# The first batch of a fused attention and MLP kernel: V by pairs, another order of steps, and copies on another engine

## The chip, the cores and the metric

The kernel runs on one core of a Trainium2 chip. A core has engines that run their own instruction streams in order: TensorE (PE in the profile; PEld is its weight load), VectorE (DVE), ScalarE (ACT), GpSimd (POOL) and SyncE (SP). They wait for each other through semaphores. Matmul results go to PSUM, which holds eight banks here; data is loaded from device memory by DMAs that POOL or SyncE issue. The metric is the device time of one execution in microseconds, as the median of several runs.

## What is computed

The reference is sparse attention, then an MLP with a squared ReLU. q, k and v are 8 x 8 x 576 x 64 (batch, head, position, channel); the first four heads look at the last 32 positions (local), the other four at the positions with the same remainder modulo 32 (strided).

```python
scores = scale * np.matmul(q, k.transpose(0, 1, 3, 2))
mask_local = (rel >= 0) & (rel < stride)
mask_strided = (rel >= 0) & (pos[None, :] % stride == pos[:, None] % stride)
scores = np.where(masks[None, :, :, :], scores, -1000000000.0)
attn = np.exp(scores - max) / sum
x = (attn @ v)                        # 4608 tokens x 512
h = x @ w_in                          # 512 x 2048
g = np.maximum(h, 0.0) ** 2
out = g @ w_out                       # 2048 x 512
```

## The kernel before, in words

Heads are worked in pairs, called units: unit u of batch b is 4b to 4b+3, the first two local, the last two strided. A unit's steps are: T, transposes of q and k on PE (TS for the strided units of the first two batches); S (`step_S`, L309), the scores with PE into four PSUM banks (two heads, called rows, by two halves of the blocks) and their exponential on ScalarE into the tile e; D (`step_D`, L405), for a local unit one part per head: e times V on PE with a column of ones beside V, a reciprocal (L434) and a product (L435) on VectorE into x_l; E (`step_E`, L438), which transposes x_l on PE and copies it to xt, the tile that the MLP reads (L464). The strided units of the first two batches use other steps in place of D and E: N (`step_N`, L378) sums e with PE and makes reciprocals with a logarithm and an exponential on ScalarE (L387, L388); O (`step_O`, L390) multiplies V by e so that the result is transposed already, and two VectorE products (L400) write xt.

The MLP takes 512 tokens at a time: `mm1` (L474) gives h for 128 columns of d_ff in four matmuls (L482), one for each 128 rows of w_in, which are the four units' channels, kk = 0 to 3; ScalarE then takes the ReLU (L488), VectorE the square (L491); `mm2` (L495) is the second matmul (L522). xt[0] and xt[1] come from the local pairs 0 and 1, xt[2] and xt[3] from the strided pairs.

No scheduler moves anything: the engines run the instructions in the order in which the program emits them (`manual_schedule`). For batch 0 that order is the list `order` in `first_steps` (L547). Each entry is a step and a number of filler matmuls (`warm`, L537) after it, whose results nobody reads. `part((kk,))` runs the matmuls of one kk for the first five column blocks of the first 512 tokens, into five banks, so that the MLP can start before all four units are done; `first_order` says which kk comes when, and in which order the first half of w_in is loaded. Later batches go by `stream_steps` (L569) and a plan of hooks, which place their loads between groups of MLP matmuls.

All early loads but the first two are on POOL's queue, in this order: q and k of unit 1 (L130), q and k of the strided units (L153), V of the local pairs (L237 for 96 of the partitions, L238 for the 32 positions before each block), V of the strided pairs (L374), and w_in (four slices at L673, then two blocks at L257). Eight semaphores serve POOL's DMAs in turn, so each issue also waits until the eighth DMA before it has landed. SyncE has its own eight.

Later in the kernel, batches 2 to 4 take their strided q and k through a cast into device memory (L165) and a transposing DMA from SyncE (L173); V of batches 2 and 3 is loaded after a small POOL copy (L605) that waits for those transposes. From batch 5 on the local q and k are loaded by SyncE (L114), cast on POOL and transposed by a DMA (L201); before that stands a DMA called hold (L609), which waits for V of batch 4.

In the list of batch 0 before the change, the part after S(2) runs: D(0,0), D(0,1), S(3), D(1,0), N(2), a filler, E(0), N(3), D(1,1), O(2), part kk=0, E(1), O(3), part kk=2, part kk=1, part kk=3.

Of the kernel before, what the change touches and what calls it, by code (L numbers as in the profile page):

```python
# [10 lines left out]
AF = mybir.ActivationFunctionType  # L11
# [3 lines left out]
def kernel(  # L15
# [9 lines left out]
    nc = tc.nc  # L25
    B, H, S, D = q.shape
# [4 lines left out]
    scale = 1.0 / (D ** 0.5)  # L31
    QL = 96
    NL = S // QL
# [25 lines left out]
    def bank(nm):  # L59
        t = banks[nm].pop(0)  # L60
        banks[nm].append(t)
        while id(t) in unread:
            run_due(lambda x: x[1] == unread[id(t)])
        return t

    unread = {}
# [3 lines left out]
    NV = 4  # L70
# [4 lines left out]
    vl_all = singles.tile([128, NV, 2, NL, VP], BF16, name="vl")  # L75
    vls = [vl_all[:, i] for i in range(NV)]
# [21 lines left out]
    st = {}  # L98

    def is_local(u):  # L100
        return units[u][1] < H // 4
# [32 lines left out]
    def cast_qk_local(u, copies, names="qk"):  # L134
        s = st[u]
        for name, copy in zip("qk", copies):
            if name not in names:
                continue
            t = qk_in.tile([QL, 6, 2, D], BF16, name=f"{name}_l")
            copy(t.rearrange("p j h d -> p h j d"),  # L140
                 s[name + "f"].rearrange("p h (j d) -> p h j d", j=6))
            s[name] = t
# [87 lines left out]
        for i in range(2):  # L230
            st.setdefault(4 * b + 2 + i, {})["vf"] = t[:, 2 * i:2 * i + 2]

    def load_v_local_sw(b):
        i = (2 * b) % NV
        t = vl_all[:, i:i + 2].rearrange("p u h t d -> p (u h t) d")[:, :, 0:D]
        src = v[b, 0:4].rearrange("h (t p) d -> p (h t) d", p=QL)
        nc.gpsimd.dma_start(out=t[32:128], in_=src)  # L237
        nc.gpsimd.dma_start(out=t[0:32, 1:4 * NL], in_=src[64:96, 0:4 * NL - 1])  # L238
        for u in range(2):
            st.setdefault(4 * b + u, {})["v"] = vls[i + u]  # L240

    def load_v_str(u, eng):
        b, p = units[u]
# [23 lines left out]
    def later(n, fn, key=None):  # L267
        pending.append((clock[0] + n, key, fn))
# [37 lines left out]
    def blk_pos(h, j):  # L306
        return NJ * (j % 2) + 4 * h + j // 2

    def step_S(u, at_once=False):  # L309
        s = st[u]  # L310
        qT, kT = s["qT"], s["kT"]
        local = is_local(u)
        w, n = (QL, NL) if local else (SP_, NJ)
        kn = 128 if local else SP_
        hn = n // 2
        e = es[u % 4]
        s["e"] = e
        pss = [[None, None], [None, None]]
        for half in range(2):
            for row in range(2):  # L320
                pss[row][half] = bank("pt")
                if u < 4:
                    bias = bias_l[:, half].rearrange("p t c -> p (t c)") if local \
                        else bias_s.rearrange("p t c -> p (t c)")
                    nc.tensor.matmul(pss[row][half][0:kn, 0:S // 2], ident[0:kn, 0:kn], bias,
                                     start=True, stop=False, skip_group_check=True)
            for i in range(hn):
                t = half * hn + i
                klo = w * t
                for row in range(2):  # L330
                    rows = slice(64 * row, 64 * row + 64)
                    if not local:
                        c0 = w * (t // 4)
                        lhsT, rhs = (a[rows, t % 4, c0:c0 + w] for a in (kT, qT))
                    else:
                        lhsT, rhs = kT[rows, klo:klo + kn], qT[rows, w * t:w * (t + 1)]
                    nc.tensor.matmul(pss[row][half][0:kn, w * i:w * (i + 1)], lhsT, rhs,  # L337
                                     start=u > 3, stop=True, skip_group_check=u < 4)

        for row in range(2):  # L340
            for half in range(2):
                unread[id(pss[row][half])] = u

        def expo(row, half):
            del unread[id(pss[row][half])]
            lo = S * row + S // 2 * half
            nc.scalar.activation(e[0:kn, lo:lo + S // 2], pss[row][half][0:kn, 0:S // 2],  # L347
                                 AF.Exp, scale=scale)

        def masks(row):  # L350
            x = e[0:kn, S * row:S * (row + 1)].rearrange("p (t c) -> p t c", c=w)
            m = mask_full if local else mask_str.to_broadcast([kn, n, w])
            nc.vector.tensor_tensor(x, x, m, op=ALU.mult)  # L353

        if u < 4:
            for half in range(2):
                for row in range(2):
                    expo(row, half)
            return
        if at_once:  # L360
            for row in range(2):
                for half in range(2):
                    expo(row, half)
            later(1, lambda: masks(0), u)
            later(2, lambda: masks(1), u)
            return
        expo(0, 0)
        later(1, lambda: expo(1, 0), u)
        later(2, lambda: expo(0, 1), u)
        later(3, lambda: (masks(0), expo(1, 1)), u)  # L370
        later(4, lambda: masks(1), u)
# [66 lines left out]
    def step_E(u):  # L438
        s = st[u]
        b, p = units[u]  # L440
        x = s["x"]
        local = is_local(u)
        n, w = (NL, QL) if local else (NJ, SP_)
        if not local and b >= XD:
            xd = dram.tile([S, 2 * D], BF16, name="x_d")
            nc.sync.dma_start(out=xd.rearrange("(p j) c -> p (j c)", j=NJ), in_=x.rearrange("p n d -> p (n d)"))
            nc.sync.dma_start_transpose(out=xt[p][:, b * S:(b + 1) * S], in_=xd)
            st.pop(u)
            return
        if local and b >= XB:  # L450
            nc.sync.dma_start_transpose(
                out=xt[p][:, b * S:(b + 1) * S].rearrange("c (t q) -> c t q", q=QL),
                in_=x.rearrange("p n d -> p (n d)"))
            st.pop(u)
            return
        px = bank("pt").bitcast(BF16)[:, 0:S]
        for t in range(n):
            nc.tensor.transpose(px[:, w * t:w * (t + 1)],  # L458
                                x[:, 2 * t:2 * t + 2, :].rearrange("p h d -> p (h d)"),
                                ident[0:w, 0:w])  # L460
        dst = xt[p][:, b * S:(b + 1) * S]
        copy = nc.scalar.copy if u < 12 else nc.vector.tensor_copy
        if local:
            copy(dst, px)  # L464
        else:
            copy(dst.rearrange("c (p j) -> c p j", j=NJ),
                                  px.rearrange("c (j p) -> c p j", j=NJ))
        st.pop(u)
# [64 lines left out]
    S_ = lambda u, at_once=False: (lambda: step_S(u, at_once or relaxed[0]))  # L533
    D_ = lambda u, part: (lambda: step_D(u, part))
    E_ = lambda u: (lambda: step_E(u))

    def warm(n):  # L537
# [3 lines left out]
                nc.tensor.matmul(pw, idle[:, 0:128], idle, start=True, stop=True)  # L541

    idle = xt[0][:, T - 512:T]
    first_order = (0, 2, 1, 3)
    NP = 5

    def first_steps():  # L547
        t, n, o = T_, (lambda u: lambda: step_N(u)), (lambda u: lambda: step_O(u))
        a, b, c, d = first_order

        def part(kks, ffs=range(NP)):
            for ff in ffs:
                mm1(0, ff, kks, first_order, None if ff < 2 else "py" if ff == 2 else "pt")

        cast1 = lambda nm: (lambda: cast_qk_local(1, (nc.vector.tensor_copy,) * 2, nm))
        v_, s_ = nc.vector.tensor_copy, nc.scalar.copy
        ts = lambda nm, half, copy: (lambda: step_TS(0, nm, half, copy))
        order = [(t(0, "q"), 2), (t(0, "k"), 2), (cast1("q"), 0), (cast1("k"), 0), (S_(0), 0),
                 (t(1, "q"), 0), (t(1, "k"), 1), (bias_strided, 0), (ts("q", 0, v_), 0), (ts("q", 1, v_), 0), (S_(1), 1),
                 (ts("k", 0, v_), 0), (ts("k", 1, s_), 1), (S_(2), 0), (D_(0, 0), 0), (D_(0, 1), 0), (S_(3), 0),  # L560
                 (D_(1, 0), 0), (n(2), 1), (E_(0), 0), (n(3), 0), (D_(1, 1), 0),
                 (o(2), 0), (lambda: part((a,)), 0), (E_(1), 0), (o(3), 0), (lambda: part((b,)), 0),
                 (lambda: part((c,)), 0), (lambda: part((d,)), 0)]
        return order

    def has_T(u):
# [37 lines left out]
    def load_v_local_gated(b):  # L604
        nc.gpsimd.tensor_copy(vl_all[64:65, (2 * b) % NV, 0, 0, 0:1], came[b])  # L605
        load_v_local_sw(b)
# [60 lines left out]
                            NEG, -NEG, op0=ALU.mult, op1=ALU.add)  # L667
    nc.vector.memset(bias_l[0:32, 0, 0], -NEG)
    load_qk_str(0, "k", room=w_out_b[:, 4:10, :])
    load_v_local_sw(0)  # L670
    load_v_str_first(0)
    for kk in first_order:
        nc.gpsimd.dma_start(out=w_in_b[:, kk, 0:1024], in_=w_in_v[:, kk, 0:1024])  # L673
# [97 lines left out]
    ts = lambda nm, half: (lambda: step_TS(1, nm, half, nc.scalar.copy if nm == "q" else nc.vector.tensor_copy))  # L771
# [82 lines left out]
```

## Time and profile before

| what | us |
|---|---|
| median of 5 runs | 308.51 |
| lowest and highest run | 308.26, 310.08 |
| profiled execution, its own time | 310.71 |
| its span, first to last instruction | 309.0 |
| PE busy, 15.0 to 18.0 / 18.0 to 20.2 / 20.2 to 23.0 | 2.84 / 1.84 / 2.64 |
| VectorE busy in the same stretches | 1.94 / 1.58 / 1.20 |
| ScalarE busy in the same stretches | 2.80 / 1.91 / 0.58 |

The granted TensorE clock was 1.00 throughout. A line of the profile names the line of the kernel, the engine, the operation, what is written from what, and how often; in the timeline the first two columns are the start and the duration (of the whole group, if several are merged), and the bracket gives the idle time before it and what ended it. In the table of waits the columns are the total, how often, and the longest.

### The profile page before, as it was taken

How to read it: one execution, taken by the hardware profiler on the slowest of the kernel's cores; microseconds unless marked ns; L12 is line 12 of the kernel's file. 1: busy time of each engine (PE TensorE's matmuls, PEld its weight loads, DVE VectorE, ACT ScalarE, POOL GpSimd, SP SyncE). 2: the span in 40 equal slices, each digit the busy share in tenths (PEclk: the TensorE clock that was granted, in tenths of full speed). 3: DMA queues.
4: the chain of work that ended last, by engine and by line, in shares of the span. 5: the costliest groups of instructions: out<-in, count | busy, mean ns of one | idle time of the engine just before them, and what ended most of it. 6: DMA issues, size and time to landing. Idle time of an engine off the chain costs nothing.

```text
span 309.0 us, 6071 instructions
## 1 busy us (share of the span) xinstructions
PE 297.5 (96%) x2326; PEld 149.8 (48%) x2368; DVE 158.5 (51%) x405; ACT 167.3 (54%) x346; POOL 74.4 (24%) x103
## 2 busy tenths in 40 slices
PE   7899999999999999899999999999999999999995
PEld 3554464545555544445444545444444444444444
DVE  4458645478677765666477577445422222222200
ACT  3768747787667765454545565555434444444311
POOL 8653400630873022722093043000000000000000
PEclk9999999999999999999999999999999999999999
DMA  8999996999999999989999783221230001000121
GB/s 161 168 207 205 189 215 126 215 194 119 133 213 88 170 202 177 200 206 220 160 231 204 192 182 88 72 55 53 75 106 35 34 34 36 34 34 36 54 82 69
DMA packets 94118, 40.75 MB, mean 132 GB/s; under 512 B 78858, under 2 KB 87754, under 8 KB 93898
## 3 DMA queue, kind: packets, MB, share of 16 engines
q0 software_dynamic: 34528, 15.00, 39.4%
q1 hardware_dynamic: 59562, 25.37, 37.1%
q8 instruction: 18, 0.29, 0.4%
q14 instruction: 10, 0.08, 0.1%
HBM read 37.64 MB, written 13.57 MB: 166 GB/s over the span
## 4 chain that ended last, share of the span: by engine, by line
PE 76%; DMA 9%; issue 6%; POOL 3%; ACT 3%; SPq 2%; DVE 1%; POOLq 0%; DVEq 0%
PE ph L482 31%; PE py L522 25%; PE ph L522 7%; PE pt L337 3%; PE pt L422 3%; DMA q_st<-in_q_dram 2%; DMA vl<-in_v_dram 2%; DMA kTl<-k_l 2%; PE pt L482 1%; DMA kT_s<-k_d 1%; DMA vl_st<-in_v_dram 1%; PE ph L504 1%; SPq L114 1%; ACT e L347 1%; PE pt L458 1%
## 5 line engine op out<-in xcount | busy, mean ns | idle before, releaser
L482 PE MATMUL ph<-xt,w_in_b 128*128 128x512 bf16 x534 | 137.7, 379 | 1.6 <-issue 0.5
L488 ACT ACTIVATE r<-ph 128x512 bf16<-128x512 f32 x138 | 82.3, 597 | 94.1 <-PE ph L482 91.2
L491 DVE TENSOR_TENSOR g_sb<-r 128x512 bf16<-128x512 bf16 x144 | 65.8, 458 | 107.1 <-ACT r L488 106.0
L522 PE MATMUL py<-w_out_b,g_sb 128*128 128x512 bf16 x385 | 100.8, 379 | 0.9 <-issue 0.2
L482 PEld LDWEIGHTS <-w_in_b 128*128 128x128 bf16 x576 | 52.4, 98 | 55.7 <-issue 0.5
L522 PEld LDWEIGHTS <-g_sb 128*128 128x128 bf16 x560 | 50.8, 98 | 54.7 <-issue 0.4
L347 ACT ACTIVATE e<-pt 72x288 bf16<-72x288 f32 (+1 forms) x128 | 45.6, 407 | 10.9 <-PE pt L337 10.9
L522 PE MATMUL ph<-w_out_b,g_sb 128*128 128x512 bf16 x139 | 34.1, 379 | 0.2
L422 PEld LDWEIGHTS <-e 128*128 128x128 bf16 (+1 forms) x384 | 20.2, 97 | 15.0 <-issue 1.0
L435 DVE TENSOR_TENSOR x_s<-pt,rinv 72x384 bf16<-72x384 f32 (+1 forms) x36 | 18.3, 509 | 1.2
L526 ACT COPY y<-py 128x512 f32<-128x512 f32 x25 | 14.6, 586 | 7.0 <-PE py L522 6.7
L435 DVE TENSOR_TENSOR x_l<-pt,rinv 96x384 bf16<-96x384 f32 x28 | 15.5, 554 | 1.0
L353 DVE TENSOR_TENSOR e<-e,mask_str 72x576 bf16<-72x576 bf16 x28 | 14.0, 510 | 3.8 <-ACT e L347 3.7
L434 DVE RECIPROCAL rinv<-pt 96x6 f32<-96x6 f32 (+2 forms) x64 | 11.8, 184 | 6.9 <-PE pt L422 6.7
L353 DVE TENSOR_TENSOR e<-e,mask_full 128x576 bf16<-128x576 bf16 x28 | 12.6, 450 | 1.9 <-ACT e L347 1.7
L422 PE MATMUL pt<-vs,e 72*128 72x65 bf16 x192 | 12.1, 193 | 0.4 <-DVE x_l L435 0.2
L220 POOL CAST vl<-vl_st 128x768 bf16<-128x768 f32 x6 | 5.4, 904 | 29.4 <-PE ph L482 16.8
L526 ACT COPY y<-ph 128x512 f32<-128x512 f32 x9 | 5.3, 584 | 13.0 <-PE ph L522 12.8
L140 POOL CAST q_l<-q_st 96x768 bf16<-96x768 f32 x6 | 5.3, 883 | 27.6 <-ACT e L347 17.5
L422 PE MATMUL pt<-vl,e 128*128 128x65 bf16 x168 | 9.8, 193 | 0.5 <-DMA vl<-in_v_dram 0.5
L617 POOL DMA_DIRECT2D vs<-in_v_dram x12 | 9.8, 819 | 1.3 <-DMA vs<-in_v_dram 1.0
L337 PEld LDWEIGHTS <-kT_s 64*72 64x72 bf16 x256 | 6.0, 113 | 7.0 <-issue 6.6
(110 smaller groups left out, 201.5 us busy)
## 6 DMA issues: line engine op xcount, KB each, us to landing
out_dram<-y SPq DMA_DIRECT2D x35, 256.0 KB, 2.8
w_out_b<-in_moe_w_out_dram POOLq DMA_DIRECT2D x4, 512.0 KB, 15.5
q_d<-in_q_dram POOLq DMA_DIRECT2D x6, 288.0 KB, 8.9
k_d<-in_k_dram POOLq DMA_DIRECT2D x6, 288.0 KB, 9.2
q_st<-in_q_dram SPq DMA_DIRECT2D x12, 144.0 KB, 4.8
k_st<-in_k_dram SPq DMA_DIRECT2D x12, 144.0 KB, 4.5
vl_st<-in_v_dram SPq DMA_DIRECT2D x12, 144.0 KB, 3.4
v_st<-in_v_dram SPq DMA_DIRECT2D x6, 288.0 KB
```

The source lines that it names most:

```text
L337: nc.tensor.matmul(pss[row][half][0:kn, w * i:w * (i + 1)], lhsT, rhs, start=u > 3, stop=True, skip_group_check=u < 4)
L347: nc.scalar.activation(e[0:kn, lo:lo + S // 2], pss[row][half][0:kn, 0:S // 2], AF.Exp, scale=scale)
L353: nc.vector.tensor_tensor(x, x, m, op=ALU.mult)
L422: nc.tensor.matmul(po[:, n - n0, :], e[0:kn, pos(n):pos(n) + 128], rhs[0:kn, src(n), 0:D + 1], start=True, stop=True)
L434: nc.vector.reciprocal(rinv[0:w, 0:m], po[0:w, 0:m, D:D + 1])
L435: nc.vector.tensor_tensor(x, po[0:w, 0:m, 0:D], rinv[0:w, 0:m].to_broadcast([w, m, D]), op=ALU.mult)
L482: nc.tensor.matmul(ph, w_in_b[:, kk, 128 * ff:128 * (ff + 1)], xt[kk][:, 512 * c:512 * (c + 1)], start=(kk == order[0]), stop=(kk == order ...
L488: nc.scalar.activation(r, ph, AF.Relu)
L491: later(1, lambda: nc.vector.tensor_tensor(g[:, ff, :], r, r, op=ALU.mult))
L522: nc.tensor.matmul(py, g[:, ff, 128 * j:128 * (j + 1)], w_out_b[:, ff, :], start=(ff == 0), stop=(ff == 15))
L526: nc.scalar.copy(y, py)
L617: nc.gpsimd.dma_start(out=t[:, NJ * i:NJ * (i + 1), 0:D], in_=v[b, h + i].rearrange("(p j) d -> p j d", j=NJ))
```

## The change

It has four parts, all in batch 0. V of the local pairs is loaded with one pair of DMAs for unit 0 and another for unit 1, in place of one pair for both. The xt copies of E(0) and E(1) run on VectorE and not on ScalarE. `step_S` can emit the exponentials of a half at once and another step between its halves; S(3) uses this to take D(0,1) between them. The list after S(2) becomes D(0,0), S(3) half 0, D(0,1), S(3) half 1, N(2), a filler, D(1,0), E(0), a filler, D(1,1), N(3), part kk=0, E(1), O(2), part kk=1, part kk=2, O(3), part kk=3; `first_order` is (0, 1, 2, 3), for the parts and for the loads of w_in.

```diff
-    def load_v_local_sw(b):
-        i = (2 * b) % NV
-        t = vl_all[:, i:i + 2].rearrange("p u h t d -> p (u h t) d")[:, :, 0:D]
-        src = v[b, 0:4].rearrange("h (t p) d -> p (h t) d", p=QL)
+    def load_v_local_sw(b, u0=0, nu=2):
+        i = (2 * b + u0) % NV
+        t = vl_all[:, i:i + nu].rearrange("p u h t d -> p (u h t) d")[:, :, 0:D]
+        src = v[b, 2 * u0:2 * (u0 + nu)].rearrange("h (t p) d -> p (h t) d", p=QL)
         nc.gpsimd.dma_start(out=t[32:128], in_=src)
-        nc.gpsimd.dma_start(out=t[0:32, 1:4 * NL], in_=src[64:96, 0:4 * NL - 1])
-        for u in range(2):
-            st.setdefault(4 * b + u, {})["v"] = vls[i + u]
+        nc.gpsimd.dma_start(out=t[0:32, 1:2 * nu * NL], in_=src[64:96, 0:2 * nu * NL - 1])
+        for u in range(nu):
+            st.setdefault(4 * b + u0 + u, {})["v"] = vls[i + u]
...
-    def step_S(u, at_once=False):
+    def step_S(u, at_once=False, between=None):
...
-        for row in range(2):
-            for half in range(2):
+            for row in range(2):
                 unread[id(pss[row][half])] = u
...
+            if between:
+                for row in range(2):
+                    expo(row, half)
+                between(half)
+        if between:
+            return
...
-        copy = nc.scalar.copy if u < 12 else nc.vector.tensor_copy
+        copy = nc.scalar.copy if 1 < u < 12 else nc.vector.tensor_copy
...
-    first_order = (0, 2, 1, 3)
+    first_order = (0, 1, 2, 3)
...
-                 (ts("k", 0, v_), 0), (ts("k", 1, s_), 1), (S_(2), 0), (D_(0, 0), 0), (D_(0, 1), 0), (S_(3), 0),
-                 (D_(1, 0), 0), (n(2), 1), (E_(0), 0), (n(3), 0), (D_(1, 1), 0),
-                 (o(2), 0), (lambda: part((a,)), 0), (E_(1), 0), (o(3), 0), (lambda: part((b,)), 0),
-                 (lambda: part((c,)), 0), (lambda: part((d,)), 0)]
+                 (ts("k", 0, v_), 0), (ts("k", 1, s_), 1), (S_(2), 0),
+                 (D_(0, 0), 0), (lambda: step_S(3, between=lambda half: None if half else step_D(0, 1)), 0), (n(2), 1),
+                 (D_(1, 0), 0), (E_(0), 1), (D_(1, 1), 0), (n(3), 0), (lambda: part((a,)), 0), (E_(1), 0),
+                 (o(2), 0), (lambda: part((b,)), 0), (lambda: part((c,)), 0), (o(3), 0), (lambda: part((d,)), 0)]
...
-    load_v_local_sw(0)
+    load_v_local_sw(0, 0, 1)
+    load_v_local_sw(0, 1, 1)
```

More of the change, by code (lines that the diff above doesn't have):

```diff
@@ L318, in step_S, with expo @@
         pss = [[None, None], [None, None]]
+        def expo(row, half):
+            del unread[id(pss[row][half])]
+            lo = S * row + S // 2 * half
+            nc.scalar.activation(e[0:kn, lo:lo + S // 2], pss[row][half][0:kn, 0:S // 2],
+                                 AF.Exp, scale=scale)
         for half in range(2):
@@ L338, in step_S @@
                                      start=u > 3, stop=True, skip_group_check=u < 4)
-        for row in range(2):
-            for half in range(2):
+            for row in range(2):
                 unread[id(pss[row][half])] = u
[L344 to L348, printed above, removed]
+            if between:
[4 more added lines that the diff above has]
+            return
         def masks(row):
```

## The prediction

> **What bounds the kernel now.** I read the page's totals first, then the timeline of 12 to 24 us, where the changed steps run, then what the matmul engine waits for after that, then the queue behind those waits.
>
> ```profile
> span 309.0 us, 6071 instructions
> PE 297.5 (96%) x2326; PEld 149.8 (48%) x2368; DVE 158.5 (51%) x405; ACT 167.3 (54%) x346; POOL 74.4 (24%) x103
> ```
>
> PE is busy 96% of the span: whatever keeps it from starting the MLP's matmuls early is paid in full, unless a later wait takes it back. The timeline of the start:
>
> ```profile
> 10.50 0.82 DVE L191 COPY qT_s<-ph 128x576 bf16<-128x576 bf16 x2 [0.33 <-PE ph L189]
> ...
> 14.09 0.54 PE L422 MATMUL ph<-vl,e 128*128 128x65 bf16 x12
> 14.10 0.68 POOL L130 DMA_DIRECT2D q_st<-in_q_dram  x1 [0.64 <-DMA g_sb<-in_v_dram]
> ...
> 14.48 0.19 DVE L434 RECIPROCAL rinv<-ph 96x6 f32<-96x6 f32 x1 [1.70 <-PE ph L422]
> 14.71 0.55 DVE L435 TENSOR_TENSOR x_l<-ph,rinv 96x384 bf16<-96x384 f32 x1
> ...
> 17.71 0.62 ACT L464 COPY xt<-pt 128x576 bf16<-128x576 bf16 x1
> ...
> 18.39 0.59 PE L482 MATMUL ph<-xt,w_in_b 128*128 128x512 bf16 x2 [0.36 <-ACT xt L464]
> ...
> 19.81 0.45 PE L398 MATMUL pt<-e,g_sb 72*64 72x72 bf16 x16
> 19.92 0.64 ACT L464 COPY xt<-pt 128x576 bf16<-128x576 bf16 x1 [0.26 <-PE pt L458]
> 20.19 8.96 PEld L482 LDWEIGHTS <-w_in_b 128*128 128x128 bf16 x43
> 20.25 1.20 DVE L400 TENSOR_TENSOR xt<-pt,g_sb 128x288 bf16<-128x288 f32 x2 [0.67 <-PE pt L398]
> ...
> 22.36 0.59 PE L482 MATMUL ph<-xt,w_in_b 128*128 128x512 bf16 x2
> ```
>
> From 14.09 on, PE goes from one step to the next. The start-to-start distances give each step's cost on PE: D half of a local pair 0.28 (15.69 to 15.98), half of S(3) 0.60 and 0.62, N 0.36, E 0.35 (19.46 to 19.81), O 0.38, a filler matmul 0.22, a part of five matmuls 5 x 0.216 = 1.08. The steps before the last part (at 22.36) sum to 7.84 with the two D halves of pair 0 back to back at 0.38; 22.36 - 14.09 = 8.27. So only 0.43 us there is waiting, 0.36 of it for the ScalarE copy of x. **No new order can gain more than about 0.4 us here**, but it can lose. What PE waits for after 23 us:
>
> ```profile
> PE pt L337 <- DMA kTl<-k_l: 1.3, 1, 1.3
> PE pt L422 <- DMA vl<-in_v_dram: 0.5, 1, 0.5
> ```
>
> The first is at 128.83, the second at 84.87. Where they come from, in the POOL and SyncE timelines and the chain:
>
> ```profile
> 36.78 0.53 POOL L165 DMA_DIRECT2D q_d<-in_q_dram  x1
> 50.98 1.39 SPq L173 DMA_TRANSPOSE qT_s<-q_d  x1
> 76.16 0.18 POOL L605 COPY vl<-kT_s 1x1 bf16<-1x1 bf16 x1 [11.57 <-DMA kT_s<-k_d]
> 77.92 6.91 DMA vl<-in_v_dram
> 105.66 0.30 SPq L609 DMA_DIRECT2D hold<-vs  x1
> 123.55 5.24 DMA kTl<-k_l
> ```
>
> q_d lands 14.1 us after its issue, at 50.88, and the transpose goes at 50.98; the next batch repeats this (63.51 + 7.3 = 70.81, transpose 70.88; gate 76.16; V issued 77.92, landed 84.82, PE at 84.87). This chain stands on landings since the start, not on PE: if PE is late, the 0.53 us wait shrinks first, and if PE were early it would grow.
>
> **The change part by part.**
> *V pair by pair.* Two DMA issues become four, with all bytes as before. One pair's issues lie between 2 x 0.68 (a DMA of few pieces, L130) and 1.21 + 0.74 (the whole loads, L237 and L238); four cost 2.7 to 3.9 against 1.95, so POOL's later issues (V of the strided pairs, six of w_in) come 0.8 to 1.95 later; I take 1.3, in the middle. The landings: K of the strided pairs 10.1, V 12.4 and 13.5, strided V 14.95, first w_in slice 16.2, six to eight us behind their issues. A queue that deep hides 1.3 us; I take 0. If the delay came through whole, the slice would land at 18.1, still before its use. Pair 0's V lands near 11.8 (half of 10.1 to 13.5), but its reader starts at 14.09 when PE gets there, so the gain is 0 to 0.05; I take 0. Each issue waits for the landing of the eighth before it: the fourth w_in slice now waits for pair 0's V and goes near 12 instead of 9.8. It landed at 20.0 and is used by the last part; 2 us later would do no harm.
>
> In rows, the 92 KB V load landed 1.1 us after the 288 KB one. The Trainium skill (DMA: Bandwidth & Descriptors, Anatomy of one DMA) fits 2.0 us plus bytes/436e3 per GpSimd DMA, and so speaks against splitting. If the two fixed parts stood in line, the first slice would land at about 20.2 and the first part would lose near 2 us, an estimate from that page. The row says they do not stand in line.
>
> *x copies on VectorE.* ScalarE loses 0.62 and 0.64. VectorE gains two copies: a contiguous one of this shape takes 0.45 (L191), a strided one 0.76 (L303). Ours is contiguous: 0.45, upper end 0.76.
>
> *The order*, worked through from 14.09 (one more filler, 0.22):
> PE: D(0,0) to 14.37, S(3) half 0 to 14.97, D(0,1) to 15.25, half 1 to 15.87, N(2) to 16.23, filler 16.45, D(1,0) to 16.73, E(0) to 17.08, filler 17.30, D(1,1) to 17.58, N(3) to 17.95.
> VectorE: a D takes 0.39 from PE's start to the reciprocal and 0.78 to the end of the product, so D(1,0) ends at 17.62; copy of x0 to 18.11; D(1,1) to 18.93.
> First part: its first matmul at 18.17 (before: 18.39), but its second takes ph_97, which D(1,1) read, so 18.99, and the part ends at 19.85. E(1) 19.85, its copy 0.46 later, 20.31 to 20.76. O(2) on PE 20.20 to 20.58. The second part now is pair 1's: 20.82 to 21.90. O(2)'s two products on VectorE are queued behind the copy, 20.80 to 22.00; third part 22.06 to 23.14. O(3) comes only then: PE 23.14, products 0.44 later, 1.20 long, to 24.78. The last part needs them and nothing stands between: PE waits from 23.52 to **24.84**.
> Against 22.36 that is **+2.5**. Strided-price copies add 0.6 (+3.1); D at 0.19, as when back to back, (0.2 less) and no gaps between engines (0.3 less) give +2.0. The old order had O(3) two parts ahead, so its 1.2 us of products was covered; now the cover is gone, and that alone is 1.3 us. ScalarE is no bound: its exponentials end near 16.6, both N near 19.4.
>
> *What later waits give back.* At 84.87 the whole 0.53, as its chain does not move: +1.95. At 128.83, 1.30 wait for the transposed K; SyncE runs without a gap from 105.66 to it, and starts when strided V of batch 4 lands. Its two last issues are held by an earlier landing at 92.88; with PE 1.95 late they move about 0.9, behind a 12 us backlog. So K is 0 to 0.9 late, the wait is taken back whole or nearly: 1.95 - 1.30 = 0.65, or 0.9. I take **+0.7**. Ends: +0.2 (2.0 - 1.83) and +2.5 (nothing given back).
>
> The profiled execution took 310.71 (span 309.0 and 1.7 around it), 2.2 over the median of the five runs; its sum is 311.4, and on the median 308.51 + 0.7 = **309.2**.
>
> **Rivals.** (a) *K's wait moves with PE*: SyncE's chain starts later with PE's use of the V buffers, and the 1.30 stays. For it: two of the V loads of batch 4 wait for PE (0.9 and 0.3 us on POOL). Then 308.51 + 1.95 = 310.5, slower. It decides once those landings move by over 1.6 us; against it, the backlog of 12 us. (b) *Nothing is given back*: the V chain at 84.87 slides too, 311.0; against it stand four transposes that start within 0.1 us of a landing. (c) *Products and copies overlap better than I chain them*, O(3)'s wait is small and x0's earlier copy counts: up to 0.4 earlier at 22.36, none of it past 84.87, where DMA holds: 308.1 to 308.5. Against it, VectorE runs in order. (d) *The whole DMA chain comes earlier*, with both later waits gone: 308.51 - 1.83 = 306.7. Against it, no byte less. (e) *The clock drops in the gaps.* It stayed 1.00 in the stretch of 126 to 132 us with 1.46 us of PE idle; the new gaps are at most 1.3. The Trainium skill (TensorE: Matmul & The Clock Gate, Part 1) puts the limit at one idle window of about 3.4 us; beyond it 3.4 us of work would cost 1.7 more, an estimate from that page.
>
> **How the numbers follow.** Forecast 0.45; (a) 0.28; (b), with the few per cent of (e), 0.13; (c) 0.08; (d) 0.06. A measurement tells about 0.5%, 1.5 us, from no change: below 307.0 is faster, above 310.05 slower. Faster is (d), 0.06; slower (a) and (b), 0.41; the rest, 0.53, is within. The forecast's own range is 308.5 to 310.0; the eight-in-ten range runs from 308.1 to 311.0, leaving out (d) and about half of (b).
>
> **What would show it.** Right: the last part starts at 24.2 to 25.4 with over 1 us of PE waiting for VectorE's L400 line before it; the second matmul of the first part waits for D(1,1); no wait for V near 86; the K wait near 129 is under 0.5. Wrong: the last part before 23.5 (order costs less), K's wait still over 1 us (rival a), or V landing later than its reader.

## The result, and the profile after

The changed kernel takes 310.47 us at the median (310.01 to 312.05) against 309.0 for the kernel before (308.09 to 313.28), measured beside each other over 54 and 94 executions: a ratio of **1.0041, 95% interval 1.0031 to 1.0051**, which is 1.3 us (the two medians lie 1.47 apart). So the change makes the kernel slower, by 0.4%, which is under the 0.5% that the forecast called no change. The median is inside the eight-in-ten range, 308.1 to 311.0, but above the forecast's own range, which ended at 310.0, and above the 310.05 from which it counted slower; its single number, 309.2, was 1.3 low. The profiled execution of the changed kernel took 310.03.

The page's totals after:

```profile
span 308.3 us, 6076 instructions
PE 296.6 (96%) x2327; PEld 149.4 (48%) x2369; DVE 159.2 (52%) x407; ACT 166.2 (54%) x344; POOL 75.3 (24%) x105
```

This span is 0.7 shorter than the 309.0 of before, although the medians stand the other way round by 1.5. One pair of profiles does not give the sign here, and the experiments say why. The timeline of the start after (start, duration, engine, line, and in the bracket the idle time before it; L427 was L422, L405 was L400, L440 was L435, L463 was L458, L469 was L464, L487 was L482, L546 was L541):

```profile
13.59 0.36 PE L427 MATMUL ph<-vl,e 128*128 128x65 bf16 x6
...
13.78 0.41 PE L332 MATMUL pt<-w_out_b,ident 72*72 72x288 bf16 x2
...
15.77 0.34 PE L427 MATMUL ph<-vl,e 128*128 128x65 bf16 x6 [0.16 <-DVE x_l L440]
...
15.95 0.42 PE L463 MATMUL pt<-ident,x_l 96*128 96x96 bf16 x6
...
16.21 0.38 PE L546 MATMUL py<-xt 128*128 128x512 bf16 x1
...
16.86 0.44 DVE L469 COPY xt<-pt 128x576 bf16<-128x576 bf16 x1
...
17.35 0.38 PE L487 MATMUL ph<-xt,w_in_b 128*128 128x512 bf16 x1 [0.21 <-DVE xt L469]
...
18.04 0.38 PE L487 MATMUL ph<-xt,w_in_b 128*128 128x512 bf16 x1 [0.31 <-DVE x_l L440]
...
18.90 0.42 PE L463 MATMUL pt<-ident,x_l 96*128 96x96 bf16 x6
...
19.36 0.46 DVE L469 COPY xt<-pt 128x576 bf16<-128x576 bf16 x1 [1.37 <-PE pt L463]
...
19.73 1.18 DVE L405 TENSOR_TENSOR xt<-pt,g_sb 128x288 bf16<-128x288 f32 x2
19.87 0.38 PE L487 MATMUL ph<-xt,w_in_b 128*128 128x512 bf16 x1 [0.17 <-DVE xt L469]
...
22.14 0.45 PE L403 MATMUL pt<-e,g_sb 72*64 72x72 bf16 x16
...
22.57 1.19 DVE L405 TENSOR_TENSOR xt<-pt,g_sb 128x288 bf16<-128x288 f32 x2 [1.66 <-PE pt L403]
...
23.81 0.59 PE L487 MATMUL ph<-xt,w_in_b 128*128 128x512 bf16 x2 [1.22 <-DVE xt L405]
```

The chain is the one that the forecast wrote down: O(3) at 22.14, its products from 22.57 to 23.76, and PE idle 1.22 us before the last part at 23.81. The second matmul of the first part waits for D(1,1)'s product (18.04, line L440). D(0,0) itself began 0.5 us sooner than in the profile of before (13.59 against 14.09), which is the start of that execution, so I count from D(0,0): the last part begins 23.81 - 13.59 = 10.22 us after it, against 22.36 - 14.09 = 8.27. **PE is 1.95 us later.** Two more profiles of the kernel before, shown further on, give 8.35 and 8.39, so 0.1 us is the noise of this measure.

Of the signs that the forecast named, PE waits over 1 us for L400 (now L405), it waits for D(1,1), and it does not wait for V or K further on. The last part itself was to start at 24.2 to 25.4. It started at 23.81, which counted from the D(0,0) of before is 14.09 + 10.22 = 24.31.

What PE waits for after 13 us (total, how often, longest; the three rows with "issue", 0.6, 0.5 and 0.2 in total, left out here):

```profile
PE ph L487 <- DVE xt L405: 1.2, 1, 1.2
...
PE ph L487 <- DVE xt L469: 0.4, 2, 0.2
PE ph L487 <- DVE x_l L440: 0.3, 1, 0.3
PE pt L427 <- DVE x_l L440: 0.2, 1, 0.2
...
PE ph L427 <- DVE x_l L440: 0.2, 1, 0.2
```

Neither the wait for V (0.53 before, at 84.87) nor the one for the transposed K (1.30, at 128.83) is there. The SyncE timeline after, for the queue behind them, and then POOL's:

```profile
50.99 2.04 SPq L173 DMA_TRANSPOSE qT_s<-q_d  x1
...
103.56 0.30 SPq L614 DMA_DIRECT2D hold<-vs  x1
...
121.50 1.22 SPq L201 DMA_TRANSPOSE kTl<-k_l  x1
```

```profile
77.04 0.18 POOL L610 COPY vl<-kT_s 1x1 bf16<-1x1 bf16 x1 [11.90 <-DMA kT_s<-k_d]
...
78.80 0.75 POOL L238 DMA_DIRECT2D vl<-in_v_dram  x1
```

The transpose at 50.99 is where it was (50.98). With PE 4.35 us late, in an experiment further on, it is at 50.51, and in two more profiles of the kernel before at 51.59 and 50.83: that chain does not follow PE. V landed at 78.80 + 6.7 = 85.50, and PE asked for it at 85.54. But hold came at 103.56, 2.1 us sooner than in the profile of before (105.66), with PE later. In the two more profiles of the kernel before it came at 103.93 and 103.71. So the lateness of 105.66 belonged to one execution.

### The profile page after: what moved, and what is told of

It reads as the page before. It is cut to its first block, busy times and chain, and to the rows that moved or that the text cites. A ratio compares the mean times of both kernels' runs of the same rounds, so it can differ in the third digit from the quotient of the medians.

```text
span 308.3 us, 6076 instructions
## 1 busy us (share of the span) xinstructions
PE 296.6 (96%) x2327; PEld 149.4 (48%) x2369; DVE 159.2 (52%) x407; ACT 166.2 (54%) x344; POOL 75.3 (24%) x105
## 3 DMA queue, kind: packets, MB, share of 16 engines
HBM read 37.63 MB, written 13.57 MB: 166 GB/s over the span
## 4 chain that ended last, share of the span: by engine, by line
PE 90%; DVE 5%; issue 2%; ACT 1%; POOL 1%; DVEq 0%; POOLq 0%
PE ph L487 37%; PE py L527 28%; PE ph L527 9%; PE pt L344 4%; PE pt L427 3%; DVE x_l L440 2%; PE pt L487 1%; PE pt L288 1%; PE pt L527 1%; PE ph L509 1%; PE pt L463 1%; DVE e L358 1%; DVE g_sb L496 1%; DVE rinv L439 0%; DVE k_l L140 0%
## 5 line engine op out<-in xcount | busy, mean ns | idle before, releaser
L487 PE MATMUL ph<-xt,w_in_b 128*128 128x512 bf16 x533 | 137.4, 379 | 3.2 <-DVE xt L405 1.2
L487 PEld LDWEIGHTS <-w_in_b 128*128 128x128 bf16 x576 | 52.4, 98 | 57.4 <-issue 2.4
L427 PEld LDWEIGHTS <-e 128*128 128x128 bf16 (+1 forms) x384 | 20.4, 97 | 14.4 <-DVE e L358 0.5
L440 DVE TENSOR_TENSOR x_s<-pt,rinv 72x384 bf16<-72x384 f32 (+1 forms) x36 | 18.3, 509 | 1.2
L440 DVE TENSOR_TENSOR x_l<-pt,rinv 96x384 bf16<-96x384 f32 x28 | 15.5, 554 | 1.0
L427 PE MATMUL pt<-vs,e 72*128 72x65 bf16 x192 | 12.1, 193 | 0.4 <-DVE x_l L440 0.2
L427 PE MATMUL pt<-vl,e 128*128 128x65 bf16 x168 | 9.7, 193 | 0.0
```

Source lines behind the costliest of these rows:

```text
L427: nc.tensor.matmul(po[:, n - n0, :], e[0:kn, pos(n):pos(n) + 128], rhs[0:kn, src(n), 0:D + 1], start=True, stop=True)
L440: nc.vector.tensor_tensor(x, po[0:w, 0:m, 0:D], rinv[0:w, 0:m].to_broadcast([w, m, D]), op=ALU.mult)
L487: nc.tensor.matmul(ph, w_in_b[:, kk, 128 * ff:128 * (ff + 1)], xt[kk][:, 512 * c:512 * (c + 1)], start=(kk == order[0]), stop=(kk == order ...
```

## The experiments

Lateness is the start of the last part of the first 512 tokens, counted from D(0,0), less the 8.27 us of before, in each profile. Ratios are to the kernel before on the same chip; "us" is the ratio times 309.

| kernel | lateness, us | ratio, 95% interval | us |
|---|---|---|---|
| changed kernel | +1.95 | 1.0041 (1.0031 to 1.0051) | +1.3 |
| O(3) one part earlier | +0.86 | 1.0017 (1.0002 to 1.0031) | +0.5 |
| eleven fillers | +2.12 and a V wait of 0.35 | 1.0067 (1.0037 to 1.0098) | +2.1 |
| twenty-two fillers | +4.35 | 1.0139 (1.0094 to 1.0184) | +4.3 |
| V by pairs alone | +0.01 | 1.0020 (0.9999 to 1.0041) | +0.6 |
| changed, V whole | +1.96 | 1.0063 (1.0040 to 1.0086) | +1.9 |
| copies alone | +0.07 and a V wait of 0.93 | 1.0009 (0.9962 to 1.0056) | +0.3 |
| changed, copies on ScalarE | +2.17 | 1.0058 (1.0039 to 1.0077) | +1.8 |
| mixed | clock disturbed | 1.0003 (0.9971 to 1.0035) | +0.1 |
| mixed, V by pairs | -0.51 | 1.0001 (0.9976 to 1.0025) | 0.0 |
| mixed, V by pairs, filler | -0.30 | 0.9987 (0.9956 to 1.0017) | -0.4 |

### O(3) one part earlier

```diff
-                 (o(2), 0), (lambda: part((b,)), 0), (lambda: part((c,)), 0), (o(3), 0), (lambda: part((d,)), 0)]
+                 (o(2), 0), (lambda: part((b,)), 0), (o(3), 0), (lambda: part((c,)), 0), (lambda: part((d,)), 0)]
```

> The changed kernel with one move: O(3) stands one part earlier, ahead of the third part and not ahead of the last. Theory (the order costs, O(3)'s 1.2 us of products have no cover): PE's wait for L405 before the last part falls from 1.22 to under 0.3 us; the last part starts about 9.1 us after D(0,0) instead of 10.2, which leaves +0.8 against the order of before (8.27); median near 309.5, 0.2% over the kernel before and about 1 us under the changed kernel. Rival (V by pairs or the copies carry the loss, the wait only moves): the last part starts 10 us or more after D(0,0) and the median stays near 310.4.

Median 309.13, ratio 1.0017. Its timeline:

```profile
21.02 0.45 PE L403 MATMUL pt<-e,g_sb 72*64 72x72 bf16 x16
21.41 0.61 PE L487 MATMUL ph<-xt,w_in_b 128*128 128x512 bf16 x2
21.46 1.19 DVE L405 TENSOR_TENSOR xt<-pt,g_sb 128x288 bf16<-128x288 f32 x2 [0.55 <-PE pt L403]
...
22.70 0.59 PE L487 MATMUL ph<-xt,w_in_b 128*128 128x512 bf16 x2
```

The products of 21.46 to 22.65 now run beside the third part on PE; the last part follows without a bracket. D(0,0) was at 13.57, so 9.13, as expected, and the median is 1.3 us under that of the changed kernel. The ratios of the two kernels to the kernel before lie 0.7 us apart. One step in the wrong place carries more than half of the loss, 1.09 of 1.95 us of lateness. The 0.86 that is left comes behind E(1). E(1) starts 5.31 us after D(0,0) in the changed kernel (18.90) and 5.37 in the old order (19.46), but there O(2) is already done. In the changed kernel it still follows, and it takes 0.62 from its start to the second part (19.25 to 19.87), the wait of 0.17 for E(1)'s copy included.

### The parts one by one

The changed kernel with V in one pair of DMAs, and the kernel before with V by pairs:

```diff
-    load_v_local_sw(0, 0, 1)
-    load_v_local_sw(0, 1, 1)
+    load_v_local_sw(0)
```

> The changed kernel with V of the local pairs loaded at once as before; order and copies stay changed. Theory: as the changed kernel, median 310.2 to 310.6, unless D(0,0) waits for the later landing (13.5 us), which would show as a PE wait of at most 0.3 us at D(0,0) that the waits further on hide. Rival (the split costs): about 0.5 to 1 us under the changed kernel.

> The kernel before with V of the local pairs loaded pair by pair, and nothing else. Theory: pair 0's V lands some 1.5 us sooner, D(0,0) still starts when PE gets there, POOL's later issues go about 1.1 us later behind a full queue: within 0.1% of before, median 308.9 to 309.2, last part 8.2 to 8.4 us after D(0,0). Rival (the split costs): the two more DMAs put the whole chain of landings up to V of batch 3 (84.8 us) later by 0.5 to 1 us and the median rises by as much, 0.2 to 0.3%.

V whole on the changed kernel: 310.62, ratio 1.0063; the last part 10.23 after D(0,0). V by pairs on the kernel before: 309.27, ratio 1.0020, its interval just reaching 1; the last part 8.28 after D(0,0). The profiled execution of the latter waited 0.2 for V, 0.6 for VectorE's x_s and 1.0 for K (at 127.72). So V by pairs is not what makes the changed kernel slow: loading V whole takes none of the lateness away. Alone, it is between nothing and +0.4%. Its median is 0.6 over the 308.67 of the kernel before on its chip, just above the expected 308.9 to 309.2 and at the lower end of what the rival said; why it rose stays open.

The xt copies alone, and the changed kernel without them (the edit is that of the second):

```diff
-        copy = nc.scalar.copy if 1 < u < 12 else nc.vector.tensor_copy
+        copy = nc.scalar.copy if u < 12 else nc.vector.tensor_copy
```

> The kernel before with the xt copies of E(0) and E(1) on VectorE, and nothing else. Theory: the first copy ends near 17.5 instead of 18.33, but the second matmul of the first part waits for D(1,1) as before (18.5), so the last part starts 8.1 to 8.3 us after D(0,0); within 0.1% of before, 308.8 to 309.1. Rival (VectorE becomes the bound): O(2)'s and O(3)'s products come later by the 0.45 us of a copy and the last part by as much, +0.3 to +0.5 us.

> The changed kernel with the xt copies back on ScalarE: order and V by pairs alone. Theory (the order costs): the wait of about 1.2 us for O(3)'s products stays, the last part starts 9.9 to 10.4 us after D(0,0), median 310.2 to 310.6. Rival (the copies on VectorE, queued between the D products, cost): the last part starts under 9.5 and the median is over 0.5 us below the changed kernel's.

Copies alone: 309.07, ratio 1.0009 with a wide interval, and five of its twelve executions took over 311.5 at a mean granted clock of 0.984 to 0.989. Its lateness without the V wait is 0.07, so VectorE did not become the bound. Order and V without the copies: 310.69 (expected up to 310.6), ratio 1.0058, and the same wait of 1.22 for O(3)'s products; in place of D(1,1)'s product, the first part now waits 0.74 for ScalarE:

```profile
18.08 0.59 PE L487 MATMUL ph<-xt,w_in_b 128*128 128x512 bf16 x2 [0.74 <-ACT xt L469]
...
22.99 1.19 DVE L405 TENSOR_TENSOR xt<-pt,g_sb 128x288 bf16<-128x288 f32 x2 [1.85 <-PE pt L403]
24.23 0.59 PE L487 MATMUL ph<-xt,w_in_b 128*128 128x512 bf16 x2 [1.22 <-DVE xt L405]
```

The order makes the loss; under it the copies are worth 0.2 us of lateness (2.17 against 1.95), twice the noise of that measure.

### Pure lateness

```diff
-                 (o(2), 0), (lambda: part((a,)), 0), (E_(1), 0), (o(3), 0),
+                 (o(2), 11), (lambda: part((a,)), 0), (E_(1), 0), (o(3), 0),
```

> The kernel before with eleven filler matmuls (11 x 0.216 = 2.38 us) between O(2) and the first part, and nothing else: they fill the 0.36 us wait for the first copy and put every later PE step about 2.0 us later, as the change did. Theory (PE's lateness is what counts, later waits give part of it back): no wait for V near 86 us and none for K near 129; median +1.2 to +1.6 over before, about what the changed kernel has. Rival (nothing is given back): +2.0, with both waits still there. Other rival (all of both waits, 1.83 us, is given back in nearly every execution): +0.2.

> As the eleven fillers, with twenty-two (4.75 us, about 4.4 net). Theory (later waits give back a bounded amount, 0.4 to 0.8 us on the median): once both are gone the rest is paid one for one, so 2.4 us over the kernel with eleven fillers, near 312.8. Rival (the start has more slack than these two waits): less than 1.5 us over it.

The edit shown is the one for eleven. They gave 310.65, ratio 1.0067; twenty-two gave 313.07, ratio 1.0139. Eleven more cost 2.4 at the medians (2.2 of lateness), one for one as expected. But the first eleven cost 2.1 of their 2.12 as well, over the expected 1.2 to 1.6 (the interval is 1.1 to 3.0, so these are not excluded), although neither later wait is in the trace. The waits after 26 us with eleven fillers:

```profile
PE pt L522 <- issue: 0.3, 2, 0.2
PE ph L482 <- issue: 0.3, 2, 0.2
PE pt L422 <- DVE x_l L435: 0.2, 1, 0.2
PE py L522 <- issue: 0.2, 1, 0.2
PE pt L422 <- DVE e L353: 0.2, 1, 0.2
```

So the waits are gone, as forecast, and yet little was given back. The profiles say how that fits. Take an execution's own time less the start of its last part. In the changed kernel that is 310.03 - 23.81 = 286.22, with twenty-two fillers 312.53 - 26.19 = 286.34. In all eight profiles that have no DMA wait after 26 us (the changed kernel, O(3) earlier, V whole, copies alone, copies on ScalarE, both with fillers, mixed) it lies between 286.22 and 286.34, whatever the order, the copies and V. In the six that have one it is 286.94 to 290.20, and 310.71 - 22.36 = 288.35 in the profile of before. **So in an execution without a later wait, lateness at the last part is paid one for one, and nothing else that the change does reaches the end.**

By this the kernel before without later waits would take 13.57 + 8.27 + 286.25 = 308.09 (D(0,0) at 13.57, as in most profiles); its fastest execution of 94 took 308.09. The changed kernel would take 310.06; its fastest of 54 took 310.01. The medians lie 0.91 and 0.46 above these. So a typical execution of the kernel before has at most about half of the 1.83 us that its first profile showed, and between the medians about 0.5 us of the 1.95 is given back (1.95 - 1.47).

### The kernel before, twice more

> The kernel before, unchanged, profiled once more. Theory (the profiled execution that the forecast rested on was 2.2 us over the median because of waits that most executions do not have): own time nearer 308.7, the wait for K at 129 us under 0.5 us, V of batch 4 landed before 104 us and not at 105.66. Rival (those waits are usual): K waits 1 us or more again, and the own time is near 310.7, so that profiling adds 2 us.

> The same once more: the wait of D(0,0) for V of the local pairs (0.0 in the first profile, 0.35, 0.93 and 0.76 in three other kernels that load V whole) and the wait for K near 129. Theory: both differ from one execution to the next; K under 0.5 us. Rival: K waits 1 us or more in every execution of the kernel before.

The own times were 310.28 and 312.15, both above the median of before, as 310.71 had been. The theory that a new profile would come out near the median missed, and so did K under 0.5 us in the first. The waits after 26 us, of the first and then of the second:

```profile
PE pt L422 <- DMA vl<-in_v_dram: 0.8, 2, 0.5
PE pt L337 <- DMA kTl<-k_l: 0.8, 1, 0.8
```

```profile
PE pt L422 <- DMA vl<-in_v_dram: 1.9, 1, 1.9
```

The sums are 1.6 and 1.9, against 1.83 in the first profile; how they divide between V and K differs each time, and K is 1.3, 0.8 and 0.0. So the rival (K 1 us or more every time) fell too. Of 94 runs of the kernel before, 12 took over 310.2 us; all three of these executions did. Either three of the longer executions were met by chance, or recording a profile itself makes the DMA chain later. The profile of the changed kernel, which has slack before these waits, came out 0.4 under its median, so a fixed cost of recording is not it. Which of the two holds is open.

The 312.15 of the second has a further cause. After its wait of 1.90 us for V the granted clock fell to 0.50 until 90 us (the matmul that ends the wait, then windows of 1 us, with the columns explained in the next section):

```profile
85.93 0.31 PE L422 MATMUL pt<-vl,e 128*128 128x65 bf16 x5 [1.90 <-DMA vl<-in_v_dram]
```

```profile
86.00:87.00 1.00, 1.00 (x16) 0.69 (x16) 0.69 (x3) 0.46 (x1) 0.79 (x2) 0.88 1.25 248
87.00:88.00 1.00, 1.00 (x9) 0.52 (x8) 0.42 (x2) 0.18 (x1) 1.00 (x2) 0.50 1.73 211
...
90.00:91.00 1.00, 1.00 (x25) 0.71 (x22) 0.23 (x2) 1.00 (x4) 0.77 (x2) 0.92 1.46 274
```

Most of the long executions go with a lower clock. Of 78 further executions of the kernel before, run beside the experiments and recorded with their clock, 14 took over 310.2 us, and 12 of these had a mean granted clock of 0.995 or less.

### Can another order win?

```diff
-                 (D_(1, 0), 0), (n(2), 1), (E_(0), 0), (n(3), 0), (D_(1, 1), 0),
+                 (D_(1, 0), 0), (n(2), 0), (E_(0), 0), (D_(1, 1), 0), (n(3), 0),
...
-        copy = nc.scalar.copy if u < 12 else nc.vector.tensor_copy
+        copy = nc.scalar.copy if 1 < u < 12 else nc.vector.tensor_copy
```

> The order of before with the xt copies on VectorE, D(1,1) ahead of N(3), and no filler after N(2): the first part no longer waits for D(1,1)'s products and O(3) keeps its two parts of cover. Theory (no order gains more than 0.4 us here, and a gain makes the wait for V near 85 us longer): last part 7.8 to 8.1 us after D(0,0), median 308.5 to 309.1, that is 0 to 0.15% under before. Rival (PE's earliness reaches the end whole): 0.3 to 0.5 us under before, and no longer V wait.

> The order of before with D(1,1) ahead of N(3), no filler after N(2), copies on VectorE, and V by pairs. Theory (V by pairs takes away D(0,0)'s wait of 0 to 0.93 us, and this order starts the last part 0.2 to 0.5 us sooner): no wait for V at D(0,0), clock 1.00 throughout, median 308.0 to 308.5. Rival (V by pairs is worth nothing, or the missing filler lets the clock drop as in the earlier profile): median 308.7 or more, or a clock of 0.5 around 18 to 22 us.

> As the last, with the filler after N(2) kept. Theory: 0.0 to 0.2 us more, as the filler's 0.22 us stands partly in a wait; median 308.1 to 308.7. Rival (the filler is what keeps the clock): clock 1.00 here and 0.5 there, and the slowest executions over 311 only without it.

The edit shown is that of mixed; the other two add V by pairs, and the last also keeps the filler after N(2). Mixed took 308.31 at the median, with a ratio of 1.0003; with V by pairs 309.04 and 1.0001; with the filler also 309.02 and 0.9987. None of the three is faster than the kernel before beyond its interval.

For the two with V by pairs the expectations (308.0 to 308.5 and 308.1 to 308.7) missed; their medians are 0.2 over the 308.80 of the kernel before on that chip. Their last part does come 0.51 and 0.30 us sooner, but in these profiles PE then waits further on. After 26 us the first waits:

```profile
PE pt L337 <- DVE x_s L435: 0.4, 1, 0.4
PE pt L288 <- DVE k_l L140: 0.4, 1, 0.4
PE pt L422 <- DMA vs<-in_v_dram: 0.2, 1, 0.2
```

and the second:

```profile
PE pt L422 <- DMA vs<-in_v_dram: 0.3, 1, 0.3
```

Mixed with V whole is not settled. Its median is 0.48 under the 308.79 of the kernel before on its chip and its profile has no DMA wait after 26 us, as the rival said. But two of its twelve executions took 311.7 and 311.9 at a clock of 0.989, which lengthen its mean. The profile of mixed shows two more things. Its windows (stretch; its length and then busy time of PE, PEld, DVE, ACT, POOL; granted clock, DMA share, GB/s):

```profile
14.00:16.00 2.00, 1.24 (x29) 0.87 (x24) 0.64 (x2) 0.82 (x3) 1.06 (x2) 1.00 1.16 209
16.00:18.00 2.00, 2.00 (x28) 1.25 (x29) 1.50 (x5) 1.99 (x6) 1.39 (x3) 0.71 1.12 206
18.00:20.00 2.00, 2.00 (x30) 1.43 (x28) 1.69 (x5) 1.82 (x5) 1.04 (x3) 0.50 1.18 205
20.00:22.00 2.00, 1.78 (x10) 0.90 (x9) 0.63 (x2) 0.29 (x1) 1.86 (x2) 0.50 1.24 206
22.00:24.00 2.00, 2.00 (x24) 1.09 (x22) 1.59 (x3) 0.00 (x0) 0.00 (x0) 0.58 1.25 204
24.00:26.00 2.00, 2.00 (x11) 0.88 (x9) 0.00 (x0) 0.19 (x1) 0.69 (x1) 1.00 1.33 210
```

The clock was at 0.50 from 18 to 22 us and between 0.50 and 1.00 on both sides of that, and the execution took 311.68. Before it stood a wait of D(0,0) for V, in the PE timeline of the same kernel and, without a fall of the clock, in that of copies alone:

```profile
14.98 0.49 PE L422 MATMUL ph<-vl,e 128*128 128x65 bf16 x11 [0.76 <-DMA vl<-in_v_dram]
```

```profile
14.73 0.49 PE L422 MATMUL ph<-vl,e 128*128 128x65 bf16 x11 [0.93 <-DMA vl<-in_v_dram]
```

Whether the gap alone did it is open: the longer gap left the clock at 1.00. The filler is not what keeps the clock: the version without it but with V by pairs kept 1.00 as well.

The clocks of all executions recorded beside the experiments point at V. Of 122 executions of kernels that load V whole, 18 had a mean granted clock of 0.99 or less (9 of 78 of the kernel before, 5 of 12 of copies alone); of 114 of kernels with V by pairs, the changed kernel's 54 among them, none had. That V by pairs prevents the fall by taking away D(0,0)'s wait is likely from this, but only one such fall at the start was traced, so the cause is argued and not shown.

## Why the prediction was right, and where it was off

**Right.** The order costs, by the mechanism named: VectorE's products of O(3) lost their cover, PE's wait before the last part is 1.22 (forecast 1.32, from 23.52 to 24.84), the second matmul of the first part waits for D(1,1), and moving O(3) back one part takes the wait away. No loss came from the copies. That the later waits are gone when PE is late is also as forecast. That an earlier start does not reach the end was borne out by the two mixed versions with V by pairs; for mixed itself it is open.

That the measured time lies in the wide range is in part luck: the lateness was put too high by 0.5 us and the give-back too high by 1.3, and the two errors offset each other in part. What they leave, 0.8 us, and a first median that was 0.5 low make up the 1.3 by which 309.2 was off.

**The +2.5 was 1.95.** The step at fault is the walk through the order: it charged D on PE 0.28 each time, and D(0,0) took 0.19 (13.59 to 13.78) and D(1,0) 0.18 (15.77 to 15.95), close to the 0.19 that it kept for its lower end; it charged E(0) 0.35, and that took 0.26 (15.95 to 16.21). By the end of the first part the walk is already 0.45 late (5.76 against 18.90 - 13.59 = 5.31); the rest comes to 0.08. The lower end, +2.0, was the better value, and still slightly high. In the sum for the old order the steps listed add up to 7.80 and not 7.84, so 0.47 and not 0.43 was waiting there. The bound of 0.4 us on what an order can gain was slightly low too: mixed with V by pairs gained 0.51, about 0.2 of it by leaving out the filler.

**The give-back of 1.83 was mis-sized.** It was read from one execution, and that execution took 2.2 us more than the median. The forecast put the 2.2 down as a difference between profile and runs and carried the waits over to the median all the same. The waits and the excess are largely the same microseconds: an execution at the median has at most about half of them, and the fastest none, so there is less for lateness to take back. Between the medians 0.5 us was given back, and between the fastest executions nothing (310.01 - 308.09 = 1.92 against a lateness of 1.95). That the first five-run median plus 1.95 gives 310.46, next to the measured 310.47, is a coincidence: that median was 0.5 below the 309.0 of the larger sample.

**The rivals.** (a), 310.5, has the right number with the wrong reason: K's wait did not move with PE, it disappeared. (b), nothing given back, is right for the fastest executions and nearer than the forecast for the typical one, though not because the V chain slides: that stayed at 50.99. (c), that copies and products overlap better, brought no gain: O(3)'s wait was 1.22, and what the walk had too much was PE's own steps. (d) did not occur, and its 306.7 took the 1.83 off a median in the same way: no execution of 94 was under 308.09. (e), the clock, stayed at 1.00 in the changed kernel with gaps up to 1.22.

**V pair by pair was costed from one landing.** The gain was put at 0 to 0.05, because D(0,0) and V's landing met in the profile of before. That was a coincidence: in eight profiled executions with V whole it landed between 13.1 and 14.9 us, and D(0,0) waited 0.35, 0.76 and 0.93 in three of them; by pairs, pair 0's landed between 11.4 and 12.8 and nothing waited. The bound should have been the spread of a landing, not the one time seen. That the split costs nothing at the landings behind it was forecast rightly: the strided V landed at 8.56 + 6.4 = 14.96, before at 14.95, the first w_in slice at 16.7 against 16.2. Over all profiles the strided V landed between 14.4 and 16.2 with V by pairs (six) and between 15.0 and 16.2 with V whole (eight), so a cost of a few tenths could not be told, but one of microseconds is not there. The Trainium skill's fixed 2.0 us per GpSimd DMA (DMA: Bandwidth & Descriptors, Anatomy of one DMA), 4 us for two more by an estimate from that page, does not show as a cost behind a queue six microseconds deep.

Whether V by pairs is worth anything in time is open. For it stand the clocks counted above. Against it stand the medians where PE is not late: V by pairs alone is 0.6 over the kernel before, mixed with it 0.2 over, and mixed without it 0.5 under. In the changed kernel V whole is 0.15 us longer at the median (310.62 against 310.47) and 0.7 by the ratios. None of these is clear of its interval.

## What to carry to other kernels

When steps of one engine's in-order list are moved, write down for each how long its result takes on the next engine and what stands between it and its reader; a producer placed directly ahead of its consumer costs that whole time. Before using waits from a profile as slack, compare that execution's own time with the median: if it is longer by about the sum of the waits, a typical execution has few of them. To see whether a change at the start reaches the end, take the own time less the start of the last step changed, and compare it between profiles with and without later waits. A DMA that lands just when it is needed in one profile may be late in others (here in three of eight), so price it by the spread of its landings.

## What the runs showed of the hardware that was not expected

The landing of the same DMA, issued at 6.70 to 6.73 us, moved over 1.8 us between executions (13.1 to 14.9). The granted clock fell to 0.50 twice in the traces: after a PE gap of 0.76 us in mixed, in a stretch where PE was busy 1.24 of 2.00 us, and after one of 1.90 us in the kernel before. The Trainium skill (TensorE: Matmul & The Clock Gate, Part 1) speaks of an idle window of about 3.4 us; both falls came after shorter gaps. Gaps of 0.93 and 1.22 in other kernels left the clock at 1.00, so the length of the gap alone does not decide it.
